# First queries loaded two tiles at a time and turned before the keys; first key copies shared between VectorE and ScalarE

## The chip, the cores and the metric

One core of a Trainium2 chip runs the whole program. The metric is the device time of one execution in microseconds (us). The profile covers the part of it from the first to the last instruction (the span), which is 1.7 to 3.5 us shorter in the runs here.

## The reference, cut to what matters

```python
def _attn_ref(q, kv, w_sr):                      # q: 4 x 12288 x 128, kv: 4 x 384 x 32 x 128
    kv_pool = kv.reshape(B, H // r, r, W // r, r, C).mean(axis=(2, 4))   # r = 4
    kv_flat = kv_pool.reshape(B, -1, C) @ w_sr   # 768 keys of a batch, also its values
    s = scale * (q @ k.transpose(0, 2, 1))
    a = np.exp(s - s.max(-1, keepdims=True)); a /= a.sum(-1, keepdims=True) + 1e-09
    return a @ v

def _moe_ref(x, w_gate, w_val, w_out):           # 49152 x 128, inner width 1536
    return (np.maximum(x @ w_gate, 0.0) * (x @ w_val)) @ w_out
```

## The kernel before

The work is done in 96 tiles of 512 queries. A long loop runs the scores of one tile, the attention values of another and the projections of a third side by side. Four tiles are a query group, with one load and one transpose by DMA; group 0 is loaded and turned in another way, as nothing can start without it.

The start makes the keys of batch 0, in three pairs of chunks. Each pair is loaded as four lines of 512 KB. TensorE sums and turns the lines by transposing matmuls (`turn_add`), the result is copied out of PSUM (`bank_ps`, to which all 9936 matmuls of the profile write), projected (`project_chunk`) and copied again. From the second pair on, VectorE adds lines 0 and 1 first (`first_lines`).

```python
    kv_load(0, 0, between=lambda: q_load_plain(0, 1))   # 2 key lines, queries of tile 0, 2 key lines
    q_load_plain(1, GRP)                                # queries of tiles 1 to 3
    for pair in range(1, NJC // 2):
        kv_load(0, pair)
    ...
    q_cast(0)
    for dh in range(3):
        for h in range(2):
            turn_add(h, line(0, dh, h), first=dh == 0)
        if dh == 1:
            fill(2); q_turn_pe(0); fill(2)
    ...                                                 # first pair: copies, products (VectorE)
    for i in range(1, GRP):
        q_cast(i)
    scores_of(0, 0)
    q_turn_pe(1)
    turn_values(0, 0)
    q_turn_pe(2)
    scores_of(1, 0)
    q_turn_pe(3)
    ...                                                 # second pair, then:
    gate = const.tile([128, 1], FP32)
    nc.gpsimd.tensor_copy(gate, line(2, 2)[:, 0, 0, 0:1])
    for own in (slice(0, D_FF // 2), slice(D_FF // 2, D_FF)):
        nc.gpsimd.dma_start(wv16[:, own], moe_w_val[:, own])
        nc.gpsimd.dma_start(wg16[:, own], moe_w_gate[:, own])
    q_load(1)                                           # query group 1
    q_turn(1)                                           # its transpose, read first by the scores of tile 4
    nc.gpsimd.dma_start(wo16, ...)
    q_load(2)
    s1 = first_lines(2)                                 # third pair's adds
    ...
```

The `gate` copy holds all of GpSimd's loads until line 2 of the third pair has landed: in the profile of the kernel before that is at 22.67 us, the copy starts at 22.72, and the first of the loads is issued at 23.63.

The softmax here doesn't subtract the row's maximum and nothing guards it: scores larger than these inputs give would overflow.

## Time and profile before

| | before |
|---|---|
| time, median of the first 3 runs | 1046.31 us (1046.07 to 1047.17) |
| span of the profiled run | 1043.4 us |
| TensorE (PE) busy | 1033.7 us, 99% |
| VectorE, ScalarE busy | 912.5 and 908.0 us, 87% each |
| line 2 of the third key pair has landed | 22.67 us |
| first value matmul of the loop starts | 31.23 us |
| transpose of query group 1 has landed | 40.83 us |
| first score matmul of tile 4 starts | 40.90 us |

In the lines of the profile PE is TensorE's matmuls, PEld its weight loads, DVE VectorE, ACT ScalarE, POOL GpSimd and SP SyncE, which issues the key lines; L153 is line 153 of that run's kernel; brackets give the idle time before an instruction and what ended it. A landing is the issue's start plus its time to landing in the trace. The last four rows are the milestones. TensorE works back to back after the start (from 45 us to the end of that profile its matmuls wait 0.8 us in all), so time won at a milestone is won at the end if nothing behind it waits longer for it. How the lines are read is shown in the prediction.

### The profile page before, as it was taken

How to read it: one execution, taken by the hardware profiler on the slowest of the kernel's cores; microseconds unless marked ns; L12 is line 12 of the kernel's file. 1: busy time of each engine (PE TensorE's matmuls, PEld its weight loads, DVE VectorE, ACT ScalarE, POOL GpSimd, SP SyncE). 2: the span in 40 equal slices, each digit the busy share in tenths (PEclk: the TensorE clock that was granted, in tenths of full speed). 3: DMA queues.
4: the chain of work that ended last, by engine and by line, in shares of the span. 5: the costliest groups of instructions: out<-in, count | busy, mean ns of one | idle time of the engine just before them, and what ended most of it. 6: DMA issues, size and time to landing. Idle time of an engine off the chain costs nothing.

```text
span 1043.4 us, 26070 instructions
## 1 busy us (share of the span) xinstructions
PE 1033.7 (99%) x9936; PEld 686.2 (66%) x9936; DVE 912.5 (87%) x1676; ACT 908.0 (87%) x1741; POOL 107.2 (10%) x127
## 2 busy tenths in 40 slices
PE   8999999999999999999999999999999999999998
PEld 5666666666666666666666666666666666666665
DVE  3788889898888888998888888999888888888898
ACT  3988888888888888888888888888888888888887
POOL 1000045100000005500000003440000000000000
PEclk9999999999999999999999999999999999999999
DMA  7843255432423335534233144561531332213111
GB/s 289 138 77 79 80 173 136 96 73 56 87 52 66 73 122 137 147 87 80 58 60 87 31 87 132 148 160 41 92 76 43 72 63 56 67 32 67 32 47 46
DMA packets 140253, 92.53 MB, mean 89 GB/s; under 512 B 117728, under 2 KB 118624, under 8 KB 140128
## 3 DMA queue, kind: packets, MB, share of 16 engines
q1 hardware_dynamic: 134544, 77.56, 29.1%
q0 software_dynamic: 5440, 13.24, 7.7%
q8 instruction: 77, 1.26, 0.5%
q14 instruction: 48, 0.39, 0.1%
q10 hardware_dynamic: 144, 0.07, 0.0%
HBM read 52.76 MB, written 25.17 MB: 75 GB/s over the span
## 4 chain that ended last, share of the span: by engine, by line
PE 95%; DMA 2%; SPq 1%; DVE 0%; issue 0%
PE bank_ps L279 24%; PE bank_ps L258 23%; PE bank_ps L269 23%; PE bank_ps L220 12%; PE bank_ps L209 11%; DMA parts<-in_kv_dram 2%; SPq L128 1%; SPq L195 1%; DMA xT<-x 0%; PE bank_ps L153 0%; PE bank_ps L173 0%; DMA kvT<-blocks 0%; DVE kv_s L372 0%; SPq L93 0%; PE bank_ps L168 0%
## 5 line engine op out<-in xcount | busy, mean ns | idle before, releaser
L272 DVE SCALAR_TENSOR_TENSOR hT<-bank_ps,val 128x512 f16<-128x512 f32 x1152 | 759.9, 687 | 100.0 <-ACT val L262 74.0
L262 ACT CAST val<-bank_ps 128x512 f16<-128x512 f32 x1152 | 678.0, 590 | 111.6 <-PE bank_ps L258 109.5
L279 PEld LDWEIGHTS <-hT 128*128 128x128 f16 x4608 | 353.2, 98 | 203.3
L279 PE MATMUL bank_ps<-wo,hT 128*128 128x128 f16 x4608 | 443.6, 219 | 0.0
L258 PE MATMUL bank_ps<-xT,wv 128*128 128x512 f16 x1152 | 436.6, 379 | 0.8 <-DVE xT L253 0.5
L269 PE MATMUL bank_ps<-xT,wg 128*128 128x512 f16 x1152 | 436.6, 379 | 0.0
L210 ACT ACTIVATE aT<-bank_ps 128x512 f16<-128x512 f32 x576 | 346.2, 604 | 17.4 <-PE bank_ps L209 17.4
L220 PE MATMUL bank_ps<-kv,aT 128*128 128x129 f16 x2304 | 223.3, 220 | 0.0
L220 PEld LDWEIGHTS <-aT 128*128 128x128 f16 x2304 | 177.3, 98 | 67.6
L209 PE MATMUL bank_ps<-qT,kv 128*128 128x512 f16 x576 | 217.3, 379 | 0.6 <-DVE qT L111 0.3
L269 PEld LDWEIGHTS <-wg 128*128 128x128 f16 x1152 | 112.7, 98 | 65.3
L258 PEld LDWEIGHTS <-wv 128*128 128x128 f16 x1152 | 112.7, 98 | 1.0 <-DMA xT<-x 0.6
L236 DVE TENSOR_TENSOR x<-bank_ps,rinv 128x256 f16<-128x256 f32 x188 | 79.7, 424 | 6.5
L78 POOL DMA_DIRECT2D q<-in_q_dram x23 | 12.5, 545 | 565.1 <-DMA qT<-q 565.0
L297 DVE TENSOR_SCALAR o_sb<-bank_ps 128x512 f32<-128x512 f32 (+1 forms) x95 | 64.0, 674 | 1.3 <-PE bank_ps L279 1.3
L139 POOL TENSOR_TENSOR s<-parts 128x512 f32<-128x512 f32 x36 | 45.3, 1269 | 164.8 <-DMA parts<-in_kv_dram 163.5
L209 PEld LDWEIGHTS <-kv 128*128 128x128 f16 x576 | 56.2, 98 | 3.3 <-issue 1.4
L228 DVE RECIPROCAL rinv<-bank_ps 128x2 f32<-128x2 f32 x192 | 30.6, 160 | 1.7 <-PE bank_ps L220 1.7
L141 POOL TENSOR_TENSOR s<-s 128x512 f32<-128x512 f32 x18 | 22.8, 1269 | 1.4
L143 POOL TENSOR_TENSOR c<-s 128x256 f32<-128x256 f32 x18 | 13.1, 727 | 1.4
L153 PEld LDWEIGHTS bank_ps<-ident,parts 128*128 128x128 f32 x64 | 7.9, 154 | 3.2 <-DMA parts<-in_kv_dram 2.3
L153 PE MATMUL bank_ps<-ident,parts 128*128 128x128 f32 x64 | 9.3, 296 | 0.7 <-DMA parts<-in_kv_dram 0.4
(43 smaller groups left out, 66.8 us busy)
## 6 DMA issues: line engine op xcount, KB each, us to landing
parts<-in_kv_dram SPq DMA_DIRECT2D x48, 512.0 KB, 6.5
out_dram<-o_sb SPq DMA_DIRECT2D x95, 256.0 KB, 2.1
q<-in_q_dram POOLq DMA_DIRECT2D x23, 512.0 KB, 5.2
kvT<-blocks SPq DMA_DIRECT2D x144, 8.0 KB, 1.8
xT<-x SPq DMA_TRANSPOSE x94, 2.5
q<-in_q_dram SPq DMA_DIRECT2D x1, 768.0 KB, 9.7
wv<-in_moe_w_val_dram POOLq DMA_DIRECT2D x2, 192.0 KB, 4.0
wg<-in_moe_w_gate_dram POOLq DMA_DIRECT2D x2, 192.0 KB, 4.9
```

Of the source, the lines that this page charges most:

```text
L139: eng.tensor_tensor(s2[:, i], parts[:, 2 * i, h], parts[:, 2 * i + 1, h], op=ALU.add)
L209: nc.tensor.matmul(s_ps, kv16[:, k // NST, jc, 0:C], qT_of(k), start=True, stop=True)
L210: nc.scalar.activation(aTs[k][:, jc, :], s_ps, AF.Exp, scale=qk_scale)
L220: nc.tensor.matmul(x_ps[:, i, :], aTs[k][:, jc, s * 128 : (s + 1) * 128], kv16[:, k // NST, jc, C : 2 * C + 1], start=(jc == 0 and i == 0) ...
L228: nc.vector.reciprocal(rinvs[k, half], x_banks[k, half][:, :, C : C + 1])
L236: nc.vector.tensor_tensor(x16s[k][:, 2 * half : 2 * half + 2, :], x_ps[:, :, 0:C], rinv.to_broadcast([128, 2, C]), op=ALU.mult,)
L258: nc.tensor.matmul(va_ps, wv16[:, fb * 128 : (fb + 1) * 128], xTs[k], start=True, stop=True)
L262: nc.scalar.copy(val, va_ps)
L269: nc.tensor.matmul(g_ps, wg16[:, fb * 128 : (fb + 1) * 128], xTs[k], start=True, stop=True)
L272: nc.vector.scalar_tensor_tensor(hTs[k][:, fb, :], g_ps, 0.0, vals.pop((k, fb)), op0=ALU.max, op1=ALU.mult)
L279: nc.tensor.matmul(o_ps, hTs[k][:, fb, s * 128 : (s + 1) * 128], wo16[:, fb, :], start=first, stop=(fb == NFB - 1), skip_group_check=True,)
L297: nc.vector.tensor_scalar(o_sb, o_ps, 1.0 / X_SCALE**2, None, op0=ALU.mult)
```

## The change

Its intent is to have tiles 0 and 1 ready when the first keys are, and to take copies off VectorE, which stands between the key lines. Cut to its core:

```diff
-    kv_load(0, 0, between=lambda: q_load_plain(0, 1))
-    q_load_plain(1, GRP)
+    kv_load(0, 0, between=lambda: q_load_plain(0, 2))
+    q_load_plain(2, GRP)
...
-    q_cast(0)
+    for i in range(2):
+        q_cast(i)
...
-            fill(2)
+            fill(3)
             q_turn_pe(0)
-            fill(2)
+            q_turn_pe(1)
+            fill(1)
     for h in range(2):
-        turn_end(h, line(0, 3, h))
+        turn_end(h, line(0, 3, h), (nc.vector, nc.scalar)[h])
     for h in range(2):
-        project_chunk(h)
-    for i in range(1, GRP):
+        project_chunk(h, (nc.vector, nc.scalar)[h])
+    for i in range(2, GRP):
         q_cast(i)
     scores_of(0, 0)
-    q_turn_pe(1)
+    scores_of(1, 0)
+    q_turn_pe(2)
+    q_turn_pe(3)
     turn_values(0, 0)
-    q_turn_pe(2)
-    scores_of(1, 0)
-    q_turn_pe(3)
...
-        turn_end(2 + h, line(1, 3, h))
+        turn_end(2 + h, line(1, 3, h), nc.scalar)
+    s1 = first_lines(2)
     for h in range(2):
         for half in range(2):
             values(0, h, half)
-        project_chunk(2 + h)
+        project_chunk(2 + h, nc.scalar)
...
     q_load(2)
-    s1 = first_lines(2)
```

It has three parts: the **loads** (first hunk), the **early turns** (casts and turns of tile 1 before the first pair ends), and the **copies** (on ScalarE, with the third pair's adds moved forward).

More of the change, by code (lines that the diff above doesn't have):

```diff
@@ L156, in turn_add, with turn_end @@
             )
-    def turn_end(chunk, lines):
+    def turn_end(chunk, lines, engine=nc.vector):
         turn_add(chunk, lines)
@@ L162, in turn_end, with project_chunk @@
         kvT = kv_Ts["pair"][:, chunk % 2]
-        nc.vector.tensor_copy(kvT, kv_Ts[chunk])
+        if engine is nc.scalar:
+            nc.scalar.copy(kvT, kv_Ts[chunk])
+        else:
+            nc.vector.tensor_copy(kvT, kv_Ts[chunk])
         kv_Ts[chunk] = kvT
-    def project_chunk(jc):
+    def project_chunk(jc, engine=nc.vector):
         pr = bank([128, 128])
         nc.tensor.matmul(pr, w_sr_f32, kv_Ts.pop(jc), start=True, stop=True)
-        nc.vector.tensor_scalar(kv16[:, 0, jc, 0:C], pr, 1.0 / (r * r), None, op0=ALU.mult)
+        if engine is nc.scalar:
+            nc.scalar.mul(kv16[:, 0, jc, 0:C], pr, 1.0 / (r * r))
+        else:
+            nc.vector.tensor_scalar(kv16[:, 0, jc, 0:C], pr, 1.0 / (r * r), None, op0=ALU.mult)
     def project(b, pair):
```

## The prediction

Three statements of how engines and queues work, which no trace shows, are cut out of it where a cut is marked. The sum is D + 0.05 us, with D at 0.4 about 0.5 us. Weight loads that follow closely start 0.05 to 0.06 us apart (40.13, 40.19, 40.24 us), and in the 0.40 us before the turns stalled until 24.42 us no other matmul runs. "Both" are the two figures 292 ns and 0.31 us. The landings of SyncE's loads come in the order of issue, from 13.75 us on 1.24 to 1.29 us apart per 512 KB; that 256 KB delay a key line by their own time is the estimate from that spacing.

> **What bounds the kernel now.** I read the busy lines and the forty slices first, then the chain that ended last, then the timeline of the first 45 us, because the change touches nothing behind them.
>
> ```profile
> PE 1033.7 (99%) x9936; PEld 686.2 (66%) x9936; DVE 912.5 (87%) x1676; ACT 908.0 (87%) x1741; POOL 107.2 (10%) x127
> PE   8999999999999999999999999999999999999998
> PE 95%; DMA 2%; SPq 1%; DVE 0%; issue 0%
> ```
>
> TensorE is busy in 99% of the span and is 95% of the chain. Everything after the start is matmuls back to back at full clock, so only TensorE idle time can be won: 1043.4 - 1033.7 = 9.7 us in all, and the stretches of five microseconds put most of it ahead of 35 us. A 2% change would be 21 us, more than twice all that idle time. The verdict is therefore nearly certain; what is open is the size inside it.
>
> The start itself is a chain of loads. The chain in order of time:
>
> ```profile
> 5.56 0.79 SPq L128
> 6.39 11.21 DMA parts<-in_kv_dram
> 17.73 2.55 PE bank_ps L153 x20
> ...
> 22.42 1.23 DVE kv_s L372
> 23.68 0.70 DVE kv_s L375
> 24.42 0.66 PE bank_ps L153 x4
> ```
>
> The reader sees that the third line of the second chunk pair lands at 17.6 us and that TensorE works on from there; then two adds on VectorE (1.23 + 0.70) stand on the chain before the third pair's turns. From the windows of 5:7.5, 7.5:10, 10:14 and 14:21 us:
>
> ```profile
> 5.00:7.50 2.50, 2.50 (x15) 2.38 (x15) 0.00 (x0) 0.00 (x0) 0.00 (x0) 1.00 0.95 267
> 7.50:10.00 2.50, 1.26 (x12) 0.75 (x11) 0.43 (x1) 0.00 (x0) 0.00 (x0) 1.00 1.04 415
> 10.00:14.00 4.00, 3.69 (x24) 2.40 (x21) 1.41 (x5) 0.00 (x0) 0.00 (x0) 1.00 1.00 414
> ```
>
> The last two figures are the DMA share and GB/s. From 7.5 us on the queue moves 412 to 415 GB/s without a break, and in 5 to 7.5 us it is as busy but moves 267. That is the slow spot: the first query load (256 KB) is issued at 2.13 and lands 7.0 us later, at 9.1, while the key line ahead of it landed at 6.4. It took 2.75 us where 256 KB at 415 GB/s are 0.63 us, so about 2.1 us are lost there. All later ones land 1.3 us apart per 512 KB (the 768 KB one 1.9 us).
>
> Further on there is a wait that no idle time shows:
>
> ```profile
> 40.24 0.42 PEld L279 LDWEIGHTS <-hT 128*128 128x128 f16 x4
> 40.62 0.10 PEld L258 LDWEIGHTS <-wv 128*128 128x128 f16 x1
> 40.87 0.10 PEld L209 LDWEIGHTS <-kv 128*128 128x128 f16 x1
> 40.90 0.10 PEld L269 LDWEIGHTS <-wg 128*128 128x128 f16 x1
> 40.90 0.38 PE L209 MATMUL bank_ps<-qT,kv 128*128 128x512 f16 x1
> ```
>
> The transpose of query group 1 is issued at 33.72 and takes 7.1 us to land: 40.83. The score matmul of tile 4 (L209), the first to read it, has its weights loaded at 40.87, 0.25 us after the load before it, where the same pair at 45.20 and 45.26 is 0.06 apart. The matmul goes at 40.90, just in its place. So the slack of that transfer against TensorE is zero already.
>
> [...] weight loads start some 0.05 us after the one before, and no matmul overtakes the stalled ones at 22.7 or 24.4 us. So scores that wait for qT stop everything behind them. [...] The trace has 292 ns for the key copies on VectorE (L163) and 2.5 us for eight 128-column ScalarE products (L234), 0.31 us each. Both say that moving a copy across saves nothing by itself. [...] The landings agree, in the order of issue, 1.3 us apart; so 256 KB put ahead of a key line delay it by their own time.
>
> **The change part by part.**
>
> Loads: 256 + 768 KB become 512 + 512 KB. The same bytes stand ahead of pair 1, so nothing changes for pairs 1 and 2 if the slow spot stays. The first pair's lines 2 and 3 get 256 KB more ahead of them: +0.63 us, line 3 lands at 11.84 + 0.63 = 12.5. If the slow spot was owed to the 2 KB pieces, up to 2.1 us come back for every later landing. Against this: the very first key packets, of 4 KB, were slow as well (GB/s in the first slices is 0, 112, then 339), so it looks like the cost of starting on a fresh tensor. I call the gain of landing time D, and expect 0 to 0.5 us.
>
> First pair: two casts (0.42 each) and two qT copies (0.42 each) on VectorE run between the query landing, about 9.8, and 11.5, ahead of line 3, so they are hidden. The second kvT copy and product on ScalarE start when TensorE ends, 12.98 and 13.6 in the old timing, where VectorE took them at 12.9 and 13.8: no gain on the path, at most 0.1. Then scores of tiles 0 and 1 follow one another, without the old 0.27 us wait for a qT copy before tile 1; TensorE reaches the second pair at about 17.0 instead of 17.3. But line 2 of that pair lands at 17.6, and the adds of L372/L375 end near 18.7 as before: the gain is waited away.
>
> Second pair: four copies (0.29 each) leave VectorE for ScalarE, which ended its eight exponentials at 19.0 and next begins at 21.6. They fit between. Path gain 0.
>
> Third pair: its adds move in front of those copies' place. Their inputs land at 21.43, so they run 21.45 to 23.4 instead of 22.42 to 24.38. TensorE is then held by line 2 (landing 22.67) and eight turns plus a score (to 23.86), and needs no wait at 24.42: the gain is 24.42 - 23.86 = 0.56 us of TensorE time.
>
> Tile 4: TensorE now comes to the L209 of 40.90 about 0.56 us earlier and meets qT landing at 40.83. Its load starts on GpSimd behind the gate, which waits for line 2 of pair 3 (22.7 us), a DMA landing that only D moves. So of 0.56 us about 0.05 stay, and the sum is D + 0.05. If D is 2 us, TensorE's own shift is 2.7 us and the sum still about D. With D at 0.4 as my middle the gain is 0.5 us.
>
> **The rivals.** First: the 2 KB pieces are the cause of the slow spot. For: it is the only load of that size and it alone is slow. Against: the 4 KB starts are slow too. Then D is about 2 and the time 1044.2. Second: the qT wait takes it all, D zero or a little negative through more contention: 1046.3, up to 1046.8. Third: qT does not hold in an ordinary run, as the profile has one execution only, and the 0.56 us stay: 1045.7. Fourth: ScalarE, full from 35 to 50 us, becomes the bound: against, it starts that stretch with the same work. I give them 20%, 35%, 25%, and 5%, the rest to sums in between.
>
> **Range and chances.** The three runs before spread over 1.1 us, so +-0.5 is noise. 1046.31 - 0.5 gives 1045.8. The low end is the first rival, 1044.2; the high end is no gain plus noise, 1046.8. Faster by 2% needs 1025.8, which is out of reach; slower by 2% needs 21 us, for which no part of the change has the work. 0.005, 0.99, 0.005.
>
> **What would show it.** In the new profile: line 2 of the third pair landing (where the gate copy on GpSimd starts) at 22.2 to 22.7; if near 20.6, the first rival. The wait of L153 for the adds (0.78 us on PEld) gone. A new idle of TensorE, 0.3 to 0.6 us, before the score matmul of tile 4 for qT; if it is missing, the third rival. Scores of tile 1 right behind tile 0. Wrong altogether would be a time under 1044 or over 1047: then a transfer that I took as fixed has moved, or a copy on ScalarE holds exponentials that TensorE waits for.

## The result

| each on its own chip | before, median (runs) | changed, median (runs) | ratio, 95% interval |
|---|---|---|---|
| first measurement | 1046.37 (6) | 1043.66 (6) | 0.9972, 0.9959 to 0.9985 |
| repeated (`after_again`) | 1044.47 (9) | 1043.42 (5) | 0.9985, 0.9972 to 0.9997 |
| repeated (`after_third`) | 1045.10 (11) | 1043.78 (6) | 0.9983, 0.9968 to 0.9998 |

A ratio is the mean time of one kernel's fast runs over the mean of the other's in the same rounds, so it is not quite the ratio of the medians. 0.9972, 0.9985 and 0.9983 are gains of 2.9, 1.5 and 1.8 us. The change is faster in all three measurements, far inside 2%; the prediction had 0.5 us, and its range ended at 1044.2. The first measurement is the odd one: the changed kernel's medians lie within 0.4 us of one another, but that of the kernel before was 1046.37 here and 1044.47 to 1045.28 later, on other chips. So the larger gain comes from slower runs of the kernel before, which nothing explains; its interval reaches down to 1.6 us.

The page of the changed kernel, busy time and the chain that ended last:

```profile
PE 1033.9 (99%) x9936; PEld 686.2 (66%) x9936; DVE 911.5 (87%) x1670; ACT 910.0 (87%) x1747; POOL 106.4 (10%) x127
PE 95%; DMA 4%; SPq 0%; POOL 0%; issue 0%; DVE 0%
```

The work is the same. DMA's share of the chain has doubled, from 2% to 4%. The windows of the changed kernel at the slow spot (the last two figures are the DMA share and GB/s):

```profile
5.00:7.50 2.50, 2.47 (x14) 2.16 (x14) 0.00 (x0) 0.00 (x0) 0.00 (x0) 1.00 1.01 318
7.50:10.00 2.50, 2.16 (x18) 1.09 (x15) 1.29 (x4) 0.00 (x0) 0.00 (x0) 1.00 1.00 392
```

The spot is still there, but moves 318 GB/s where 267 were before. The changed kernel's chain, in order of time (start, length, what):

```profile
11.25 10.23 DMA parts<-in_kv_dram
...
21.53 0.19 POOL gate L429
...
23.90 8.30 DMA q<-in_q_dram
...
32.21 7.64 DMA qT<-q
...
39.90 0.39 PE bank_ps L215
```

And its weight loads at tile 4:

```profile
38.94 0.10 PEld L264 LDWEIGHTS <-wv 128*128 128x128 f16 x1
39.90 0.10 PEld L215 LDWEIGHTS <-kv 128*128 128x128 f16 x1 [0.86 <-DMA qT<-q]
```

In this execution the chain is what the prediction described: landing of the third pair, gate, load and transpose of query group 1, scores of tile 4. TensorE idles for the transpose, 0.86 us at the weight load. Against 40.90 us the score matmul starts 1.0 us earlier, of 1.7 us that TensorE had won at the first value matmul (31.23 to 29.55). In the two later profiles of the same kernel this wait is nearly absent, which the experiments show.

### The profile page after: what moved, and what is told of

Read it like the earlier page. It is cut to its first block, busy times and chain, and to the rows that moved or that the text cites. A ratio compares the mean times of both kernels' runs of the same rounds, so it can differ in the third digit from the quotient of the medians.

```text
span 1042.1 us, 26069 instructions
## 1 busy us (share of the span) xinstructions
PE 1033.9 (99%) x9936; PEld 686.2 (66%) x9936; DVE 911.5 (87%) x1670; ACT 910.0 (87%) x1747; POOL 106.4 (10%) x127
## 3 DMA queue, kind: packets, MB, share of 16 engines
q8 instruction: 77, 1.26, 0.5%
## 4 chain that ended last, share of the span: by engine, by line
PE 95%; DMA 4%; SPq 0%; POOL 0%; issue 0%; DVE 0%
PE bank_ps L285 25%; PE bank_ps L264 24%; PE bank_ps L275 24%; PE bank_ps L226 12%; PE bank_ps L215 11%; DMA parts<-in_kv_dram 2%; DMA q<-in_q_dram 1%; DMA qT<-q 1%; DMA xT<-x 0%; PE bank_ps L179 0%; SPq L128 0%; POOL wv L431 0%; POOL wg L432 0%; SPq L93 0%; DVE o_sb L303 0%
## 5 line engine op out<-in xcount | busy, mean ns | idle before, releaser
L78 POOL DMA_DIRECT2D q<-in_q_dram x23 | 12.5, 544 | 567.5 <-DMA qT<-q 567.4
```

## The experiments

Two numbers are taken from each profile: when line 2 of the third pair lands (L), and when the first value matmul of the loop starts (V). From V to tile 4's scores TensorE takes 9.66 us wherever nothing is waited for (nine of the 18 profiles); what a profile shows above that is the wait there. L does not hold V directly in the kernel before, whose chain goes by the second pair's landing at 17.60 us and the adds (see the prediction); but the landings behind the first query loads move together (in the first profiles of both kernels they come 1.24 to 1.29 us apart per 512 KB from 13.8 us on), so V - L compares the kernels. Theory A: the loads move L, the moved adds shorten V - L, and a later wait may take some of it. Theory B: the order of the instructions decides. There were sixteen runs beside the first two, on four chips; each has its own runs of the kernel before. The intervals of the timed ratios overlap for all parts of the change, so the timed runs do not tell the parts apart: that rests on the profiles.

### One part at a time

`loads_only` is the kernel before with the first hunk of the diff. `copies_only` is it with the copies and the moved adds, without the other two parts.

```diff
-    kv_load(0, 0, between=lambda: q_load_plain(0, 1))
-    q_load_plain(1, GRP)
+    kv_load(0, 0, between=lambda: q_load_plain(0, 2))
+    q_load_plain(2, GRP)
```

> The kernel before with the query loads of the change alone (512 + 512 KB in place of 256 + 768 KB). Theory A (the loads decide: the first query load loses less time at its slow spot, all later landings and with them the gate and the transpose of query group 1 come earlier, and tile 4's scores wait for that transpose): line 2 of the third pair lands 1.0 to 1.5 us earlier than in the kernel before (22.67 us), no wait of over 0.2 us at tile 4's scores, and nearly the whole gain of the change: 2 us or more in the timed runs. Theory B (the order of the instructions and the copies on ScalarE decide): under 0.7 us of gain.

Measured: 1044.69 us median against 1045.12, ratio 0.9993 (0.9980 to 1.0007). L was 21.86 us, 0.81 earlier than in the first profile of the kernel before, but V only 31.03. The loads move the landing, and TensorE does not get it. The chain of `loads_only` shows why:

```profile
13.68 0.29 DVE kv L169
13.97 1.00 DVE q16s L101 x3
14.98 0.34 DVE qT L111
...
16.55 1.23 DVE kv_s L372
17.80 0.70 DVE kv_s L375
18.55 1.53 PE bank_ps L153 x12
```

Products, casts, query copies and the second pair's adds follow one another on VectorE, while the lines 0 and 1 that those adds read had landed at 14.20 and 15.48 us. VectorE's queue has become the bound. It starts from line 3 of the first pair, which with the new loads has 256 KB more ahead of it and landed at 11.63 us, only 0.21 earlier than before (11.84); V comes 19.4 us after that line in both kernels. Neither theory had this.

```diff
 # copies_only, against the kernel before
-        turn_end(h, line(0, 3, h))
+        turn_end(h, line(0, 3, h), (nc.vector, nc.scalar)[h])
-        project_chunk(h)
+        project_chunk(h, (nc.vector, nc.scalar)[h])
-        turn_end(2 + h, line(1, 3, h))
+        turn_end(2 + h, line(1, 3, h), nc.scalar)
+    s1 = first_lines(2)                 # taken from its place after q_load(2)
-        project_chunk(2 + h)
+        project_chunk(2 + h, nc.scalar)
```

> The kernel before with the copies on ScalarE and the third pair's adds moved forward, but with the old loads and the old order of casts and turns. Theory A: the landings stay (line 2 of the third pair at 22.5 to 22.8 us), TensorE comes to tile 4's scores about 0.56 us earlier and waits 0.4 to 0.6 us there for the transpose of query group 1, so the time stays within 0.4 us of the kernel before. Theory B: a gain of 0.5 us (the wait for the adds taken away) to 2 us.

Measured: 1043.73 against 1045.12, ratio 0.9986 (0.9973 to 0.9999). L was 22.44, V 30.52, so V - L is 8.08 us where it was 8.56. The 0.48 us are a wait of TensorE for the third pair's adds, which is gone. TensorE's first turns of that pair and those that read the adds, in the kernel before and then in `copies_only`:

```profile
22.71 1.09 PE L153 MATMUL bank_ps<-ident,parts 128*128 128x128 f32 x8
24.42 0.66 PE L153 MATMUL bank_ps<-ident,kv_s 128*128 128x128 f32 x4 [0.40 <-DVE kv_s L375]
22.49 1.09 PE L153 MATMUL bank_ps<-ident,parts 128*128 128x128 f32 x8 [0.32 <-DMA parts<-in_kv_dram]
23.70 0.60 PE L153 MATMUL bank_ps<-ident,kv_s 128*128 128x128 f32 x4
```

The adds began at 22.42 us in the kernel before, behind a copy of VectorE at 22.21, and at 21.28 here, though the lines that they read had landed at 21.43 and 21.19. No run moves the adds and leaves the copies, so what the copies add to this is not shown. Theory A's wait at tile 4 did not come, although TensorE was 0.71 us early: the transpose landed at 39.75. The ratio, 1.5 us, is compatible with 0.5 us and with more.

`loads_turns` is the changed kernel without the copies and moved adds; `loads_copies` is `copies_only` with the new loads, that is, the changed kernel with the old order of casts and turns.

```diff
 # loads_turns, against the changed kernel
-        turn_end(h, line(0, 3, h), (nc.vector, nc.scalar)[h])
+        turn_end(h, line(0, 3, h))
-        project_chunk(h, (nc.vector, nc.scalar)[h])
+        project_chunk(h)
-        turn_end(2 + h, line(1, 3, h), nc.scalar)
-    s1 = first_lines(2)
+        turn_end(2 + h, line(1, 3, h))
-        project_chunk(2 + h, nc.scalar)
+        project_chunk(2 + h)
+    s1 = first_lines(2)                 # in its old place
```

> The changed kernel without its copies on ScalarE and without the third pair's adds moved forward: the loads and the early casts and turns alone. Seen so far: the first value matmul of the loop starts at 31.23 us in the kernel before, 31.03 with the loads alone, 30.52 with the copies alone, 29.55 and 29.53 in the changed kernel, so the parts do not add up (0.2 + 0.7 against 1.7). If the missing part is that with the loads alone VectorE's own queue (one cast and one query copy more between the first pair and the adds of the second) holds the earlier landing back: the first value matmul here starts 8.4 to 8.7 us after line 2 of the third pair has landed (8.56 in the kernel before, 9.17 with the loads alone), at 29.7 to 30.5 us, and the timed gain is 0.7 to 1.3 us. If the early turns do nothing: near 31.0 us, and a gain under 0.5 us.

Measured: 1044.24 against 1044.98, ratio 0.9995 (0.9982 to 1.0008); L 21.29, V 29.87, V - L 8.58. As expected in the profile: with the early turns VectorE is free in time, and the loop starts as soon after the landing as in the kernel before. The timed gain, 0.5 us by the ratio, fell short of the 0.7 expected, within its interval; in the profile 0.37 us went to the wait at tile 4.

> The kernel before with the new loads, the copies on ScalarE and the moved adds, but with the old order of casts and turns. VectorE's queue is then shorter by one copy and one product behind the first pair (0.58 us of work), so it should hold the second pair's adds back less than with the loads alone: first value matmul at 29.7 to 30.3 us, between the changed kernel and the others. At 30.8 us or later the early turns are the needed part.

Measured: 1042.91 against 1044.98, ratio 0.9990 (0.9973 to 1.0006), one of six runs being at 1047.75 us; L 21.31, V 29.38, V - L 8.07. It is as early as the changed kernel (the two were not timed on one chip), so the early turns aren't needed once the copies have left VectorE. What matters is that one of the two parts relieves VectorE (V was 29.87 and 29.38 us with one of them, 31.03 with the loads alone). There is no slack in it here: the chain of this profile still runs through the second pair's adds (15.74 us).

### The landing, and chance

> The changed kernel once more, unedited, on the chip of this call: a second profile of it and the size of its gain beside runs of the kernel before on the same chip. If the first measurement (0.9972, or 2.9 us) is typical: 2 to 3.5 us of gain. If the gain is what the two profiles show (the spans differ by 1.3 us): 0.8 to 1.8 us.

Measured (changed kernel, unedited): ratio 0.9985; L 21.47, V 29.53, V - L 8.06. At tile 4:

```profile
39.07 0.10 PEld L215 LDWEIGHTS <-kv 128*128 128x128 f16 x1
```

No idle time is noted there: the transpose landed at 39.02 us, and the matmul started at 39.19 in step with those ahead of it. Yet the span was only 0.3 us shorter than in the first profile of this kernel; the rest was lost behind tile 4 (1002.6 us from there to the end, against 1002.2).

> The kernel before, unedited, as a run of its own: ratio 1.000 within 0.13%, and a second profile of it. In the four profiles with its 256 KB query load, line 2 of the third pair landed at 21.7 to 22.7 us (mean 22.4), in the eight with the 512 KB load at 20.7 to 22.3 (mean 21.5). If the loads are what wins 0.9 us, it lands at 22.0 to 22.8 here; at 21.5 or earlier the difference is rather chance. The first value matmul starts 8.5 to 8.6 us after that landing in every kernel with VectorE's copies and the adds in their old place.

Measured (kernel before, unedited): ratio 0.9994 (0.9976 to 1.0012), so two means of one kernel differ by 0.06% here. L 22.56, V 31.11, V - L 8.55, as expected; but with the loads alone it had been 9.17, so "every kernel" was too wide. The timeline of its gate copy, which starts 0.05 us after L, of V and of tile 4's weight load:

```profile
22.61 0.95 POOL L421 COPY gate<-parts 128x1 f32<-128x1 f32 x1 [20.59 <-DMA parts<-in_kv_dram]
31.11 0.38 PE L258 MATMUL bank_ps<-xT,wv 128*128 128x512 f16 x1 [0.52 <-DVE xT L253]
41.18 0.10 PEld L209 LDWEIGHTS <-kv 128*128 128x128 f16 x1 [0.58 <-DMA qT<-q]
```

> The changed kernel, unedited, once more: the gain was 2.9 us in the first measurement and 1.5 us in the second. From the profiles I expect 0.9 us (landing) and 0.5 us (adds), less 0 to 0.7 us for the transpose's wait, and so 0.7 to 1.8 us here. First value matmul 8.05 to 8.1 us after line 2 of the third pair has landed. A gain of over 2.5 us would say that something beside these counts which the profiles don't show.

Measured (changed kernel, unedited): 1043.78 against 1045.10, ratio 0.9983 (0.9968 to 0.9998). The same three instructions:

```profile
21.41 0.19 POOL L429 COPY gate<-parts 128x1 f32<-128x1 f32 x1 [19.39 <-DMA parts<-in_kv_dram]
29.43 0.38 PE L264 MATMUL bank_ps<-xT,wv 128*128 128x512 f16 x1 [0.52 <-DVE xT L259]
39.13 0.10 PEld L215 LDWEIGHTS <-kv 128*128 128x128 f16 x1 [0.22 <-DMA qT<-q]
```

The reader sees the gate 1.20 us earlier than in `before_again` and the first value matmul 1.68 us earlier, so 0.48 are the adds. The kernel before waits for the transpose in this profile too (0.58 against 0.22 us): what looked like a toll on the changed kernel is paid by both, sometimes.

Over all profiles with the 256 KB load between key lines 1 and 2 (five), L was 22.67, 22.56, 22.44, 21.69 and 22.68, mean 22.41. With the 512 KB load there (ten) it was 20.71 to 22.29, mean 21.45. The difference of 0.96 us is over twice the standard deviation of either set (0.4 us), though the sets overlap: one profile with the 512 KB load has 22.29. The loads win the landing on average, not in every execution.

### The wait for the transpose of query group 1

`after_early_q1` and `before_early_q1` put that group's load and transpose ahead of the second halves of the weights.

```diff
         nc.gpsimd.dma_start(wg16[:, own], moe_w_gate[:, own])
-    q_load(1)
-    q_turn(1)
+        if own.start == 0:
+            q_load(1)
+            q_turn(1)
```

> The changed kernel with the load and the transpose of query group 1 put ahead of the second halves of the two weight matrices. Theory A: the transpose lands 2 to 3 us earlier (about 37 us), the wait of 0.70 us ahead of tile 4's scores is gone, and it is 0.6 to 0.8 us faster than the changed kernel. If the wait was not what held TensorE there, or the weight halves now come too late (they are needed near 33 us, and would land near 32), the time stays or gets worse.

> The kernel before with the same earlier load of query group 1. Theory A: the wait there is just touched (0.25 us between two weight loads, no idle time of TensorE), so the gain is 0 to 0.1 us: the wait of tile 4 only counts once the work ahead of it has become faster. A gain of over 0.5 us would say that the ordinary runs of the kernel before wait there more than its profiled run.

Measured: 1043.83 and 1045.31 against 1045.12, ratios 0.9982 (0.9969 to 0.9996) and 0.9993 (0.9980 to 1.0006). The expectation for the transpose failed: it was issued 2.8 us earlier (29.4 us) than in the changed kernel and landed no earlier (40.26 us). The timeline of the DMA queue's issues in `after_early_q1`:

```profile
29.43 7.42 SPq L88 DMA_TRANSPOSE qT<-q  x1
```

The weight loads of the same profile at tile 4:

```profile
40.30 0.10 PEld L215 LDWEIGHTS <-kv 128*128 128x128 f16 x1 [1.82 <-DMA qT<-q]
```

The issue alone took 7.42 us (4.76 in the kernel before), and TensorE, which had come earlier, idled more. In `before_early_q1` the transpose landed at 40.13. So in these kernels the transpose ends 1.5 to 3.5 us after the load of query group 2 (37 to 39 us), whenever it is issued. `after_q2_late` and `after_q2_late_b` (the same kernel, on two chips) hold that load back:

```diff
+    gate2 = const.tile([128, 1], FP16)
+    nc.gpsimd.tensor_copy(gate2, qTs[1][:, 0, 0:1])
     q_load(2)
```

> The changed kernel, with the load of query group 2 on GpSimd held until the transpose of group 1 has landed. In the six profiles so far that transpose landed between 39.8 and 40.8 us, 1.7 to 3.5 us after the load of group 2 had landed, even where it was issued at 29.4 us. If that load is what delays it: the transpose lands before 38 us, the wait ahead of tile 4's scores (0.70 us in the changed kernel's profile) is gone, and it is about 0.7 us faster than the changed kernel. If the transpose waits for something else, it lands near 40 us again and the wait stays.

> The changed kernel with the load of query group 2 held until the transpose of group 1 has landed, once more and beside the changed kernel on the same chip: no wait ahead of tile 4's scores, its transpose landed before 38.5 us, and 0.2 to 0.7 us faster than the changed kernel in the mean of the runs (0.5 us in the first pair of measurements, within their noise).

Measured: the transpose landed at 37.81 and 36.60 us, 4.8 and 4.5 us after its issue (beside the load of group 2 it took 7.1 in the kernel before, 7.6 in the changed kernel and 10.8 in `after_early_q1`), and tile 4's scores don't wait. The load of group 2 was what delayed it. From the timeline of `after_q2_late_b`, weight loads 0.06 us apart:

```profile
38.90 0.10 PEld L264 LDWEIGHTS <-wv 128*128 128x128 f16 x1
38.96 0.10 PEld L215 LDWEIGHTS <-kv 128*128 128x128 f16 x1
```

The time hardly follows: 1043.06 us median beside 1043.42 for the changed kernel on the first chip (means 1042.95 and 1043.49), 1043.94 beside 1043.78 on the second. That fits the two profiles of the changed kernel from those chips, with 0.0 and 0.05 us of TensorE time lost to the wait. A version that takes the wait away is not measurably faster than the changed kernel.

### The slow spot

The loss is the time between the landing ahead and that of the query load, less its bytes at 415 GB/s, the rate of the kernel before in 7.5 to 10 us (0.63 us for 256 KB, 1.26 for 512 KB). Between key lines 1 and 2 the 256 KB load lost 1.3 to 2.2 us (mean of five profiles 1.8), the 512 KB load 0.3 to 1.6 us (mean of ten 0.9). The difference of 0.9 us is that of the landings, so it is here that the loads win. Five kernels looked for the cause.

```diff
 # after_touch, before_touch: one early load of 64 KB of the queries
     nc.scalar.dma_start(w_sr_f32, w_sr)
+    touch = const.tile([128, C], FP32)
+    nc.scalar.dma_start(touch, q[0, 0 : GRP * T, :].rearrange("(p s) c -> p s c", p=128)[:, 0])
 # after_split: two loads of 256 KB in place of the one of 512 KB
-    kv_load(0, 0, between=lambda: q_load_plain(0, 2))
+    kv_load(0, 0, between=lambda: (q_load_plain(0, 1), q_load_plain(1, 2)))
```

> The changed kernel with one small load (64 KB, 512 bytes of each of the 128 partitions' queries) put first, behind that of the projection matrix on ScalarE's queue. Theory 'cold tensor': the first query load then loses next to nothing, 1.3 to 1.5 us between the landing of the line ahead and its own (1.94 us in the changed kernel), and all later landings come 0.3 to 0.6 us earlier. Theory 'position or burst' (the third load of the queue is slow whatever it reads): no change beyond 0.3 us.

> The kernel before with the same small early load. Theory 'cold tensor': the 256 KB query load lands 0.6 to 1.0 us after the line ahead of it instead of 2.8 us, and line 2 of the third pair at 20.5 to 21.3 us instead of 22.7. Theory 'small pieces' (2 KB pieces are slow by themselves) or 'position': it stays at 1.9 to 2.8 us.

Measured: 1043.90 and 1045.48 against 1044.47, ratios 0.9991 (0.9978 to 1.0004) and 1.0004 (0.9991 to 1.0018). The query load still landed 1.75 and 2.16 us behind the line ahead, a loss of 0.5 and 1.5 us, and line 1 itself came 0.2 to 0.7 us later with the extra load. The theory of the cold tensor is not borne out: both losses lie within those of the other kernels.

> The changed kernel with the first query load made as two of 256 KB, each with pieces of 2 KB per partition, in the place of one of 512 KB with pieces of 4 KB. What was lost at the slow spot so far (time from the landing of the line ahead to that of the query load, less its bytes at 415 GB/s): 1.3 to 2.2 us, 1.7 in the mean of four profiles, for the 256 KB load; 0.3 to 1.6 us, 0.8 in the mean of six, for the 512 KB one. If small pieces cost the time, the loss over both loads here is 2.5 us or more. If the loss is one for the group, whatever its size, and is partly covered by a longer load: 0.3 to 1.6 us over both.

Measured, one run: 1043.48 us. The first 256 KB landed 2.07 us behind the line ahead, the second 0.82 behind it: losses of 1.4 and 0.2 us. Small pieces by themselves do not explain it, as the second load has them too and took 0.82 us, where its bytes at 415 GB/s are 0.63. The packets in the trace of the kernel before say the same: those of the query load, 2 KB each, took 84 ns in the median where 4 KB take 159, so per byte they are 6% slower only; but one in ten took over 320 ns. Part of the loss is in such slow packets (what the 128 packets took beyond 84 ns each comes to 8.5 us, 0.53 us for each of 16 DMA engines); what slows them is not shown. The sum of 1.6 us is at the top of what was expected for one loss per group.

`before_late_q0` puts the 256 KB load behind key line 2, `before_q_last` behind key line 3.

```diff
-            if dh == 1 and between is not None:
+            if dh == 2 and between is not None:      # before_late_q0
 # before_q_last
-    kv_load(0, 0, between=lambda: q_load_plain(0, 1))
+    kv_load(0, 0)
+    q_load_plain(0, 1)
```

> The kernel before with its 256 KB query load put behind the third key line in place of the second. If the slow spot belongs to the place in the queue (the third load): the third key line lands 2.3 us or more behind the second (1.28 us at full rate) and the query load 0.6 to 0.9 us behind it. If it belongs to the query load: the third key line comes 1.3 us behind the second, the query load 1.9 to 2.8 us behind that.

> The kernel before with its first query load behind all four key lines of the first pair, for the slow spot alone (it is slower, as the first scores wait for that load). If the spot is bound to the third place in the queue or to that time: line 2 lands 1.8 to 2.8 us behind line 1 and the query load within 1 us of line 3. If it is bound to the query tensor: lines 2 and 3 land 1.3 us apart each, and the query load 1.9 to 2.8 us behind line 3.

Measured, one run each: 1046.16 and 1048.10 us. V came at 32.44 and 33.63 us, as the first scores get their queries later; a single run does not show how much slower the kernels are (1046.16 lies within the runs of the kernel before). Key line 2, now third in the queue, landed 1.77 and 1.73 us behind line 1, a loss of 0.5 us each time; the query load then lost 0.7 us in the fourth place and 0.3 us in the fifth. Neither theory holds alone: the third place cost a key line 0.5 us, and the 256 KB query load there lost more (1.3 to 2.2 us). Nor is it the query load alone that is slow at that time: in 5 to 7.5 us `before_q_last` has nothing but key lines to load and moves 338 GB/s, against 412 in 14 to 21 us of the profile of the kernel before. Why the 512 KB load loses less than the 256 KB one stays open.

## Why the prediction was wrong, point by point

**Right.** The verdict (within 2%), the milestones, and their order: landings of the third pair, the adds, the transpose of group 1. The adds' gain was put at 0.56 us and measured 0.48 to 0.49. A kvT copy took much the same on either engine: 266 ns on ScalarE (group row of the changed kernel's page below) and 292 on VectorE in the kernel before. The prediction's figure of 0.31 us for ScalarE's products is their busy time shared out; one took 374 ns. The first rival, an earlier landing, was on the list with 20%, but for a reason, the 2 KB pieces, that `after_split` speaks against. And the sign that it named for being wrong, a time under 1044 because a transfer taken as fixed has moved, is what came.

```profile
L164 ACT COPY kvT<-bank_ps 128x128 f32<-128x128 f32 x3 | 0.8, 266 | 11.0 <-PE bank_ps L153 11.0
```

**Wrong: the size of D.** The step was "I call the gain of landing time D, and expect 0 to 0.5 us", with 0.4 as the middle. In the unedited kernels D was 22.61 - 21.43 = 1.18 us (means of two and three profiles), and 0.96 over all kernels with these loads. The argument was that a slow start would recur and cost the same. It recurs, but took 0.7 to 0.9 us in the three profiles of the changed kernel instead of 2.1. Likewise "line 3 lands at 11.84 + 0.63 = 12.5": it landed at 11.23.

**Wrong, the slack at tile 4: "of 0.56 us about 0.05 stay".** The transpose wait took 0.70 us of TensorE time in one profile of the changed kernel, 0.0 and 0.05 in the others, and 0.41 in the second profile of the kernel before. One profile had shown zero slack, and I read it as a fixed limit. Its landing moves from run to run with the load of group 2 (39.86 and 39.02 us in two profiles of the changed kernel). The third rival, that the wait does not hold in an ordinary run, describes the adds' gain better.

**Missing: the parts need each other.** The prediction let D pass to TensorE whole. With the loads alone it does not: V came only 0.20 us earlier with L 0.81 earlier, as VectorE's queue held the second pair's adds. Either the early turns or the copies free it.

The corrected sum is D 1.18 + adds 0.49 = 1.67 us at the first value matmul, and 1.63 us at tile 4's scores (means of the profiles: 41.04 against 39.41). The two repeated measurements have 1.5 and 1.8 us. The first one's 2.9 us are more than the profiles explain; its interval holds 1.67, and I can't show any further cause.

## What to carry to other kernels

In a start bound by a queue of loads, follow the landings by name and ask of each part of a change whether it moves a landing or the work behind it: a moved landing is only worth what the engines behind it can follow (with the loads alone, 0.20 us of 0.81). A stall seen in one profile is one draw (the loss at the 256 KB query load was 1.3 to 2.2 us in five profiles, the wait for the transpose 0.0 to 0.70 us in three of one kernel); before a prediction rests on its size, it needs several profiles, and so does a transfer with no slack. Gains of 0.1% want repeats on several chips: one gave 2.9 us, the next two 1.5 and 1.8.
